# A row maximum that reaches all partitions through ScalarE copies and a vector transpose, in a gated attention kernel

## The chip, the core and the metric

The kernel runs on one core of a Trainium2 chip. A core has five engines that run their own instruction streams side by side: TensorE (PE, matrix products into PSUM banks), VectorE (DVE), ScalarE (ACT), GpSimd (POOL) and SyncE (SP, which here only issues DMA transfers). Each stream is executed in its order; semaphores make one engine wait for another. The metric is the device time of one execution in microseconds (us), as the median of several runs.

## The reference

All data are float32. `x` is 2048 x 640, with 32 heads of width 128; `W` is 512, so each head sees the last 512 keys.

```
xn = layernorm(x)
q  = xn @ wq                                  # 32 heads
p  = softmax(q k^T * Dh**-0.5)                # k, v: the last 512 rows of the cache
s  = (p v) @ wo
h  = relu(xn @ w1 + b1) ** 2                  # 640 -> 1728
g  = silu(h @ w2 + b2)
return x + s * g
```

## The kernel before

Every matrix product is made of three: each operand is split into a high part, rounded to the matmul's input type, and the low remainder, and high x high, high x low and low x high are summed (`triple`). So each tensor that goes into a product needs a rounding copy (on ACT) and a subtraction (on DVE or POOL).

The kernel first runs the norm and the MLP of the gate (`first_step` over 14 chunks of the hidden width for the first of four row tiles, then pairs of chunks for two more, then the products with `w2`); pieces that are needed later are stored to DRAM ("spills": `xT_d`, `ts_d`, the gate `g_d`, the hidden tiles `h_m`). The fourth row tile's MLP is computed at the end (`late_*`).

Then comes attention: 128 **units**, one for each pair of a head and a tile of 512 rows; `hf` counts two halves of 64 units, each with two row tiles, and in the second half the projection of q is computed with fewer products by sums of weight blocks. For unit `i`:

- `s_mm`: scores, transposed: four PSUM banks `s` (one for 128 keys each), 128 keys on the partitions, 512 rows along the free axis. The four banks serve one unit at a time.
- `max_fold`: the maximum over the keys. DVE reads each bank transposed in blocks of 32x32 and takes the maximum over 32 keys; the result `rdm` holds, on 4 x 32 partitions, partial maxima. `gather` copies three groups of 32 partitions to the first (ACT), and `row` reduces them to 32x16, `rowm`.
- In the kernel before, SP then stores `rowm` to DRAM (`m_d`) and loads it back onto all 128 partitions (`bm`, 128x512).
- `shift`: `e = s - bm`, four instructions on DVE, which free the banks of `s`.
- `expo` and `p_hi` (ACT), `p_lo` (POOL) twice each, for two halves of 128x1024 in `e`: the exponential and its two parts `pt`.
- `s_add` (POOL) adds the two halves of `e`, `s_fold` (DVE, `rds`) reduces them over keys; gather, `sq`, its reciprocal and a transpose `rows` follow. This row goes through DRAM too (`s_d`, `bs`), before and after the change.
- `v_mm`: the product with v, into `o`; `o_norm` multiplies by `bs`; `o_hi` and `o_lo` split the result into `ot`.
- Every second unit the heads' outputs are multiplied by `wo` in five blocks (`r_mm`), and `r_acc` adds them to `acc` on DVE.

The order is written out by hand. The calls of all units are put into one list, `plan`, each with a planned time (`on(10.4 + 0.4 * c, shift, i, c)` means 10.4 us after the unit's start, units being 12.4 us, `PERIOD`, apart); the list is sorted by that time and executed, and each engine runs its instructions in exactly that order. So a number in the list sets only the order on an engine, not a time. `BM` and `BS` are the planned times within a unit for DMA issues on SP.

After the last unit the rest of the fourth tile's MLP runs, mixed with the finishing of the second half's outputs: `load_finish` loads a gate tile `fg` and an input tile `fx` (two buffers each), `finish_gate` multiplies on DVE, `finish` adds on POOL or DVE and, before the change, stores the output on SP's queue at once.

Of the kernel before, what the change touches and what calls it, by code (L numbers as in the profile page):

```python
# [25 lines left out]
def kernel(  # L26
# [729 lines left out]
    def first_step(f):  # L756
# [142 lines left out]
    def raw_tile(kind, name):  # L899
        if "fin" in pools and kind in "vsxgw":  # L900
            n = D if kind == "w" else W
            return pools["fin"].tile(
                [P, n], F32, tag=f"fin{kind}", name=name, bufs=1 if kind in "vw" else 2
            )
# [225 lines left out]
    def max_fold(i, c):  # L1130
        if c == 0:
# [3 lines left out]
            SC[i, c].rearrange("p (i b) -> p b i", i=B32),  # L1135
# [10 lines left out]
    def row(i, what):  # L1146
        rd = RD.pop((i, what))[:B32].rearrange("p b a c -> p b (a c)")
        r = ap.tile([B32, B32], F32, tag="row", name=f"row{what}{i}", bufs=4)
        if what == "m":
            r = r[:, :NQ]  # L1150
            dve.tensor_reduce(r, rd, axis=AX.X, op=ALU.max)
        else:
            sq = SQ[i % len(SQ)]
            dve.tensor_reduce(sq[:, :NQ], rd, axis=AX.X, op=ALU.add)
            dve.reciprocal(sq[:, :NQ], sq[:, :NQ])
            dve.transpose(r, sq)
            r = r[:NQ]
# [4 lines left out]
        (MB if what == "m" else RB)[i] = bc  # L1162
# [319 lines left out]
    for p in range(1, NP):  # L1482
# [142 lines left out]
    BM, BS = 4.4, 11.9  # L1625
    for n in range(NG):
# [13 lines left out]
        for k, lo, what, *places in (  # L1640
# [8 lines left out]
            (3, 2, "s4", (2, BM), (2, BS)),  # L1649
# [5 lines left out]
    for t in range(TPH):  # L1655
        at((b - 5 + t * G) * PERIOD + 4.3, open_xT, 1, t)
    for u, when, pieces in (
# [3 lines left out]
        (-5, BM, ((0, 2),)),  # L1661
        (-5, BS, ((0, 3),)),
        (-4, BM, ((0, 0),)),
        (-4, BS, ((0, 1),)),
        (-3, BM, ((0, 4),)),
        (-3, BS, ((1, 0), (1, 1))),
        (-2, BM, ((1, 2),)),
        (-2, BS, ("t31", (1, 3))),
        (-1, BM, ((1, 4),)),
        (-1, BS, ("t40", "t41x")),  # L1670
# [39 lines left out]
    for i in range(NU):  # L1710
# [21 lines left out]
        if NG <= n < HALF * NG:  # L1732
# [29 lines left out]
            if n > NG:  # L1762
                at(t0 - PERIOD + 4.4, q_piece, n, slot)
# [15 lines left out]
        on(PERIOD + 8.5, row, i, "s")  # L1779
        on(18.6, p_lo, i, 1)  # L1780
        for c in range(KC):
            on(PERIOD + 8.5 + 0.68 * c, v_mm, i, c)
        on(2 * PERIOD + (4.15 if i >= NQS and i % UPG == UPG - 2 else 3.6), o_norm, i)
        on(2 * PERIOD + 4.9, o_hi, i)
        on(2 * PERIOD + 5.5, o_lo, i)
        if i % G == G - 1:
            for d in range(DC):
                last = i == NU - G - 1
                if i < NU - 1:
# [14 lines left out]
                    if k == "x" and round(when % PERIOD, 2) in (7.5, 7.75) and not last:  # L1804
                        done = when - when % PERIOD + 12.5
                    on(done, r_acc, i, d)
                if g == NG - 1 and hf == 0:
                    at((i + ((4, 4, 5, 5, 5), (4, 4, 4, 5, 5))[t][d]) * PERIOD + 4.3, store_acc, t, d)
                    w = (NU // 2 + 9 + 4 * d) * PERIOD
                    if t == 0:  # L1810
# [3 lines left out]
                        at(w + 3 * PERIOD - 0.7, finish, 0, t, d)  # L1814
    z = (NU - 1) * PERIOD
# [92 lines left out]
    at(z - 3 * PERIOD + 4.3, open_xT, HALF, 0)  # L1908
    for c in range(DC):
        for i in range(2):  # L1910
            when = ((4.5, 11.9), (16.9, 16.95), (24.3,) * 2, (24.3,) * 2, (29.2,) * 2)[c][i]
# [56 lines left out]
```

## Time and profile before

| | us |
|---|---|
| three timed runs | 2039.5, 2040.52, 2040.64 |
| median | 2040.52 |
| profiled execution | 2033.68 |
| its span, first to last instruction | 2031.9 |

| engine | busy share of the span |
|---|---|
| POOL | 67% |
| ACT | 62% |

The profile is one execution. A line of its order in time gives the start, the length, the engine, the operation with "written tile <- read tiles", and in brackets how long the engine had stood idle before and what released it. Attention fills the stretch from about 300 to 1930 us. The granted TensorE clock is 0.992 over the span.

### The profile page before, as it was taken

How to read it: one execution, taken by the hardware profiler on the slowest of the kernel's cores; microseconds unless marked ns; L12 is line 12 of the kernel's file. 1: busy time of each engine (PE TensorE's matmuls, PEld its weight loads, DVE VectorE, ACT ScalarE, POOL GpSimd, SP SyncE). 2: the span in 40 equal slices, each digit the busy share in tenths (PEclk: the TensorE clock that was granted, in tenths of full speed). 3: DMA queues.
4: the chain of work that ended last, by engine and by line, in shares of the span. 5: the costliest groups of instructions: out<-in, count | busy, mean ns of one | idle time of the engine just before them, and what ended most of it. 6: DMA issues, size and time to landing. Idle time of an engine off the chain costs nothing.

```text
span 2031.9 us, 29531 instructions
## 1 busy us (share of the span) xinstructions
PE 1961.2 (97%) x8489; PEld 1586.2 (78%) x8489; DVE 1638.8 (81%) x2851; ACT 1249.6 (62%) x2226; POOL 1368.6 (67%) x771
## 2 busy tenths in 40 slices
PE   9999999999999999999999999999999999999977
PEld 7887887788888888877877777777777777777765
DVE  6873747898989988899888778888888888888753
ACT  5665537766666666666665576666666666666522
POOL 1022108888888888888886677777777777777631
PEclk9999999999999999999999999999999999999988
DMA  6567945444444444444444544444444444444363
GB/s 211 189 236 270 360 170 169 138 142 141 137 136 139 141 141 137 146 146 146 136 147 136 177 135 143 143 143 142 140 123 123 123 126 126 128 125 140 110 221 130
DMA packets 196126, 315.57 MB, mean 155 GB/s; under 512 B 28212, under 2 KB 85062, under 8 KB 194694
## 3 DMA queue, kind: packets, MB, share of 16 engines
q1 hardware_dynamic: 192102, 297.54, 46.8%
q0 software_dynamic: 3728, 15.99, 2.0%
q8 instruction: 77, 1.26, 0.2%
q14 instruction: 75, 0.61, 0.1%
q10 hardware_dynamic: 144, 0.16, 0.0%
HBM read 243.08 MB, written 70.53 MB: 154 GB/s over the span
## 4 chain that ended last, share of the span: by engine, by line
PE 41%; DMA 20%; DVE 18%; POOL 10%; ACT 6%; issue 4%; SPq 1%; DVEq 0%; ACTq 0%; POOLq 0%
DMA bm<-m_d 9%; PE r L78 7%; PE pq L78 7%; PE py L78 7%; PE s L78 7%; DVE e L78 6%; POOL pt L78 6%; PE o L78 5%; DVE rdm L78 4%; POOL e L78 4%; DMA m_d<-rowm 4%; PE ph L78 3%; DMA bs<-s_d 2%; DVE acc L78 2%; ACT pt L78 2%
## 5 line engine op out<-in xcount | busy, mean ns | idle before, releaser
L78 POOL TENSOR_TENSOR pt<-e,pt 128x1024 fp32r<-128x1024 f32 x256 | 615.6, 2405 | 271.7 <-ACT pt L78 271.1
L78 PE MATMUL r<-ot,wo 128*128 128x512 f32 x1920 | 492.7, 390 | 2.6 <-DVE acc L78 1.7
L78 ACT ACTIVATE e<-e 128x1024 f32<-128x1024 f32 x256 | 269.5, 1053 | 262.0 <-DVE e L78 256.7
L78 PEld LDWEIGHTS r<-ot,wo 128*128 128x128 f32 x1920 | 360.3, 188 | 80.2 <-DVE acc L78 3.0
L78 PE MATMUL s<-q,wk 128*128 128x512 f32 x1536 | 375.4, 393 | 27.2 <-DVE e L78 26.7
L78 PE MATMUL o<-pt,wv 128*128 128x512 f32 x1536 | 381.8, 393 | 7.1 <-POOL pt L78 4.3
L78 DVE TENSOR_TENSOR e<-s,bm 128x512 f32<-128x512 f32 x512 | 317.1, 680 | 73.6 <-DMA bm<-m_d 68.4
L78 PEld LDWEIGHTS s<-q,wk 128*128 128x128 f32 x1536 | 284.1, 188 | 103.8 <-issue 32.3
L78 PEld LDWEIGHTS o<-pt,wv 128*128 128x128 f32 x1536 | 284.3, 188 | 83.4 <-POOL pt L78 26.1
L78 DVE TRANSPOSE_TENSOR_REDUCE rdm<-s 128x16 f32<-128x512 f32 x512 | 324.3, 685 | 5.0 <-PE s L78 4.9
L78 POOL TENSOR_TENSOR e<-e,e 128x1024 f32<-128x1024 f32 x128 | 308.6, 2411 | 10.0
L78 ACT ACTIVATE pt<-e 128x1024 fp32r<-128x1024 f32 x256 | 271.8, 1062 | 6.9
L78 PE MATMUL pq<-ax,wq 128*128 128x512 f32 x960 | 228.0, 389 | 0.0
L78 PEld LDWEIGHTS pq<-ax,wq 128*128 128x128 f32 x960 | 180.2, 188 | 37.4
L78 DVE TRANSPOSE_TENSOR_REDUCE rds<-e 128x32 f32<-128x1024 f32 x128 | 159.5, 1246 | 58.6 <-POOL e L78 58.1
L78 DVE TENSOR_TENSOR acc<-r,acc 128x512 f32<-128x512 f32 x300 | 201.8, 673 | 3.1 <-PE r L78 3.0
L78 ACT ACTIVATE rdm<-rdm 32x64 f32<-32x64 f32 x384 | 97.8, 255 | 133.5 <-DVE rdm L78 130.1
L78 ACT ACTIVATE rds<-rds 32x32 f32<-32x32 f32 x384 | 90.0, 234 | 82.1 <-DVE rds L78 77.7
L78 POOL TENSOR_TENSOR wo<-or,wo 128x640 fp32r<-128x640 f32 x62 | 104.9, 1691 | 8.0 <-ACT wo L78 7.9
L78 DVE TENSOR_TENSOR o<-o,bs 128x512 f32<-128x512 f32 x128 | 87.3, 682 | 21.3 <-DMA bs<-s_d 20.6
L78 PE MATMUL py<-ch,cw 128*128 128x512 f32 x410 | 95.9, 395 | 4.8 <-ACT r L78 4.8
L78 DVE TENSOR_TENSOR ot<-o,ot 128x512 fp32r<-128x512 f32 x128 | 86.9, 679 | 15.6 <-ACT ot L78 14.3
(460 smaller groups left out, 2492.6 us busy)
## 6 DMA issues: line engine op xcount, KB each, us to landing
bm<-m_d SPq DMA_DIRECT2D x128, 256.0 KB
bs<-s_d SPq DMA_DIRECT2D x128, 256.0 KB
or<-in_wo_dram SPq DMA_DIRECT2D x62, 320.0 KB
qp<-wq_d SPq DMA_DIRECT2D x30, 640.0 KB
kr<-in_kT_dram SPq DMA_DIRECT2D x62, 256.0 KB
vr<-in_v_dram SPq DMA_DIRECT2D x62, 256.0 KB
wq_d<-ss SPq DMA_DIRECT2D x60, 256.0 KB
qp<-wq_d SPq DMA_DIRECT2D x30, 512.0 KB
```

Source lines behind the costliest of these rows:

```text
L78: ins = method(*args, **kwargs)
```

## The change

Three things are changed.

First, the maximum no longer goes through DRAM. `row` writes `rowm` into the first 32 of 128 partitions; three ACT copies (`copies`) repeat it on the other three groups of 32; and one DVE instruction (`across`) transposes, in 32x32 blocks, a 128x512 pattern in which each of the 16 columns is read 32 times, so that every partition ends with all 512 maxima. The block order that `max_fold` reads is changed to fit.

Second, the planned times in the list are changed around this: the subtractions, exponentials and copies come earlier, the fold of the sum moves ahead of the row of the maximum, and the split of `o` and some loads and stores of projection weights (`BM`, `BS`) move.

Third, the spills of the MLP's inputs (`xT_d` of two tiles) are issued earlier, only part of the second is spilled, and the temporary sums `ts_d` are spread over four steps; the output stores are taken out of `finish` and put later into the list.

```
-        if p in (2, 3):
-            spill(p - 1, XS[p - 1])
-        for k in {1: (0,), 4: (1, 2), 5: (3,)}.get(p, ()):
+        if p < NP - 1:
             for i in range(2):
-                pool.dma_start(TS_d[k][:, :, i, :], raw(TS[k][i]))
+                pool.dma_start(TS_d[p - 1][:, :, i, :], raw(TS[p - 1][i]))
...
+        if f in (9, 10):
+            pool.dma_start(xT_d[T1][f - 9], raw(XS[T1][f - 9]))
+        if f == FC - 1:
+            cs = slice(NQ2, DC)
+            for i in range(2):
+                pool.dma_start(xT_d[T2][i][:, cs, :], raw(XS[T2][i])[:, cs, :])
...
-            SC[i, c].rearrange("p (i b) -> p b i", i=B32),
+            SC[i, c].rearrange("p (b i) -> p b i", i=B32),
...
     def row(i, what):
         rd = RD.pop((i, what))[:B32].rearrange("p b a c -> p b (a c)")
+        if what == "m":
+            r = MR[i] = ap.tile([P, NQ], F32, tag="rowm", name=f"rowm{i}", bufs=2)
+            dve.tensor_reduce(r[:B32], rd, axis=AX.X, op=ALU.max)
+            return
...
+    def copies(i):
+        for a in range(1, P // B32):
+            act.activation(MR[i][a * B32 : (a + 1) * B32], MR[i][:B32], AF.Copy)
+
+    def across(i):
+        MB[i] = ap.tile([P, NT], F32, tag="bm", name=f"bm{i}", bufs=1)
+        dve.transpose(
+            MB[i].rearrange("p (b i) -> p b i", i=B32),
+            MR.pop(i)[:, :, None].to_broadcast([P, NQ, B32]),
+        )
...
         (pool if t == hf else dve).tensor_tensor(a, a, FX.pop(("x", hf, t, d)), op=ALU.add)
-        store(sp, hf, t, d, a)
+        FX["o", hf, t, d] = a
+
+    def finish_store(hf, t, d):
+        store(sp, hf, t, d, FX.pop(("o", hf, t, d)))
...
-    BM, BS = 4.4, 11.9
+    BM, BS = 0.85, 4.5
...
         on(3.95, gather, i, "m")
         on(4.1, row, i, "m")
+        on(4.25, copies, i)
+        on(7.0, across, i)
         for c in range(KC):
-            on(10.4 + 0.4 * c, shift, i, c)
-        on(11.7, expo, i, 0)
-        on(12.7, p_hi, i, 0)
-        on(13.8, expo, i, 1)
-        mid = i >= NQS and i % UPG == UPG - 1
-        on(PERIOD + (4.0 if mid else 5.2), p_hi, i, 1)
-        on(13.9, p_lo, i, 0)
-        on(16.2, s_add, i)
-        on(PERIOD + 6.2, s_fold, i)
-        on(PERIOD + 8.0, gather, i, "s")
-        on(PERIOD + 8.5, row, i, "s")
-        on(18.6, p_lo, i, 1)
+            on(8.2 + 0.6 * c, shift, i, c)
+        on(9.5, expo, i, 0)
+        on(10.6, p_hi, i, 0)
+        on(10.7, expo, i, 1)
+        on(10.9, p_hi, i, 1)
+        on(11.0, p_lo, i, 0)
+        on(11.1, s_add, i)
+        on(11.2, p_lo, i, 1)
+        on(PERIOD + 3.5, s_fold, i)
+        on(PERIOD + 4.15, gather, i, "s")
+        on(PERIOD + 4.4, row, i, "s")
...
-        on(2 * PERIOD + (4.15 if i >= NQS and i % UPG == UPG - 2 else 3.6), o_norm, i)
+        on(2 * PERIOD + 4.2, o_norm, i)
         on(2 * PERIOD + 4.9, o_hi, i)
-        on(2 * PERIOD + 5.5, o_lo, i)
+        on(2 * PERIOD + (7.6 if i < NU - 1 else 5.5), o_lo, i)
...
             at(z + 36.0 + 4.0 * t + 8.0 * d, finish, HALF - 1, t, d)
+            at(z + 46.0 + 4.0 * t + 8.0 * d, finish_store, HALF - 1, t, d)
```

The matmuls on PE stand in the same order before and after. On DVE, in the first half, this stood between the fold of the sum of unit 27 (`rds27`) and the first two subtractions of unit 28 (`e28_0`); the digits after the tile's name are the unit, then the half of `e` or the bank of `s`:

```order
L78 TENSOR_REDUCE rds27_6962<-e27_0_6875 128x2x16
L78 SCALAR_TENSOR_TENSOR q30_1_6977<-pq30_6943,q30_0_6976 128x512
L78 TENSOR_REDUCE sq3_2985<-rds27_6962 32x16
L78 RECIPROCAL sq3_2985<-sq3_2985 32x16
L78 STREAM_TRANSPOSE rows27_6992<-sq3_2985 32x32
L78 TENSOR_TENSOR e28_0_7014<-s28_0_6893,bm28_6940 128x512
L78 TENSOR_TENSOR e28_0_7014<-s28_1_6902,bm28_6940 128x512
```

In the changed kernel the same place on DVE reads:

```order
L78 TENSOR_REDUCE rds27_6967<-e27_0_6877 128x2x16
L78 TENSOR_REDUCE rowm28_6972<-rdm28_6941 32x16
L78 TENSOR_TENSOR acc0_0_3561<-r25_1_6959,acc0_0_3561 128x512
L78 TENSOR_TENSOR o26_6889<-o26_6889,bs26_6848 128x512
L78 TENSOR_REDUCE sq3_2985<-rds27_6967 32x16
L78 RECIPROCAL sq3_2985<-sq3_2985 32x16
L78 STREAM_TRANSPOSE rows27_6986<-sq3_2985 32x32
L78 STREAM_TRANSPOSE bm28_7005<-rowm28_6972 128x512
L78 TENSOR_TENSOR ot26_6994<-o26_6889,ot26_6994 128x512
L78 TENSOR_TENSOR e28_0_7019<-s28_0_6931,bm28_7005 128x512
L78 SCALAR_TENSOR_TENSOR q30_1_7017<-pq30_6982,q30_0_7016 128x512
L78 TENSOR_TENSOR e28_0_7019<-s28_1_6937,bm28_7005 128x512
```

`rowm`, `acc`, `o` and `ot` have moved from ahead of `rds` to behind it, `bm` is new, and the second part of q has moved between the two subtractions.

On ACT, in the second half, this stood between the exponential of unit 92's second half and that of unit 93's first:

```order
L78 ACTIVATE e92_1_15806<-e92_1_15806 128x1024
L78 ACTIVATE rdm93_15824<-rdm93_15824 32x16x4 x3
L78 ACTIVATE ot91_15869<-o91_15786 128x512
L78 ACTIVATE pt92_1_0_15871<-e92_1_15806 128x1024
L78 ACTIVATE q94_0_15884<-pq23b_15637 128x512
L78 ACTIVATE q95_0_15888<-pq23a_15790 128x512
L78 ACTIVATE rds92_15881<-rds92_15881 32x16x2 x3
L78 ACTIVATE wv1_13_0_15902<-vr1_13_15798 128x512
L78 ACTIVATE e93_0_15927<-e93_0_15927 128x1024
```

In the changed kernel ACT's order there is:

```order
L78 ACTIVATE e92_1_15892<-e92_1_15892 128x1024
L78 ACTIVATE pt92_1_0_15908<-e92_1_15892 128x1024
L78 ACTIVATE rdm93_15924<-rdm93_15924 32x16x4 x3
L78 ACTIVATE rds92_15949<-rds92_15949 32x16x2 x3
L78 ACTIVATE rowm93_15960<-rowm93_15960 32x16 x3
L78 ACTIVATE ot91_15978<-o91_15881 128x512
L78 ACTIVATE q94_0_15986<-pq23b_15739 128x512
L78 ACTIVATE q95_0_15990<-pq23a_15887 128x512
L78 ACTIVATE wv1_13_0_16006<-vr1_13_15899 128x512
L78 ACTIVATE e93_0_16004<-e93_0_16004 128x1024
```

The gather of the sum (`rds92`) and the three new copies of `rowm93` now stand ahead of `ot91` and of the first parts of q.

More of the change, by code (lines that the diff above doesn't have):

```diff
@@ L902, in raw_tile @@
             return pools["fin"].tile(
-                [P, n], F32, tag=f"fin{kind}", name=name, bufs=1 if kind in "vw" else 2
+                [P, n], F32, tag=f"fin{kind}", name=name, bufs={"v": 1, "w": 3}.get(kind, 2)
             )
@@ L1147, in row @@
         rd = RD.pop((i, what))[:B32].rearrange("p b a c -> p b (a c)")
+        if what == "m":
+            r = MR[i] = ap.tile([P, NQ], F32, tag="rowm", name=f"rowm{i}", bufs=2)
+            dve.tensor_reduce(r[:B32], rd, axis=AX.X, op=ALU.max)
+            return
         r = ap.tile([B32, B32], F32, tag="row", name=f"row{what}{i}", bufs=4)
[L1149 to L1157, printed above, removed]
+        sq = SQ[i % len(SQ)]
+        dve.tensor_reduce(sq[:, :NQ], rd, axis=AX.X, op=ALU.add)
+        dve.reciprocal(sq[:, :NQ], sq[:, :NQ])
+        dve.transpose(r, sq)
+        r = r[:NQ]
         d = dpool.tile(list(r.shape), F32, tag=f"{what}_d", name=f"{what}_d{i}", bufs=4)
@@ L1161, in row @@
         sp.dma_start(bc, d.rearrange("a b -> (a b)")[None, :].to_broadcast([P, NT]))
-        (MB if what == "m" else RB)[i] = bc
+        RB[i] = bc
+    MR = {}
+    def copies(i):
[7 more added lines that the diff above has]
+        )
     def shift(i, c):
@@ L1660 @@
         (-14, BM, ("t30",)),
[L1661 to L1670, printed above, removed]
+        (-5, BS, ((0, 2),)),
+        (-4, BM, ((0, 3),)),
+        (-4, BS, ((0, 0),)),
+        (-3, BM, ((0, 1),)),
+        (-3, BS, ((0, 4), (1, 0))),
+        (-2, BM, ((1, 1),)),
+        (-2, BS, ("t31", (1, 2))),
+        (-1, BM, ("t41x", (1, 3))),
+        (-1, BS, ("t40",)),
+        (0, BM, ((1, 4),)),
         (1, BS, ("t41",)),
```

13 lines of the change are left out of this document (6 added, 7 removed).

## The prediction

> **What bounds the kernel now.** I read the busy shares first, then the waits, then the order in time of one unit of attention (a head times a tile of 512 rows; 128 of them follow one another). "L78" is the line of a wrapper through which every instruction is issued, so I go by tile names: `s` scores, `rdm`, `rowm`, `bm` the maximum in its three forms, `e` exponentials, `pt` their two parts, `rds`, `sq`, `rows`, `bs` the sum, `o`, `ot` the head's output, `acc` the accumulator, `sw` sums of projection weights.
>
> ```profile
> PE 1961.2 (97%) x8489; PEld 1586.2 (78%) x8489; DVE 1638.8 (81%) x2851; ACT 1249.6 (62%) x2226; POOL 1368.6 (67%) x771
> DVE rds L78 <- POOL e L78: 58.1, 103, 3.0
> DVE e L78 <- DMA bm<-m_d: 68.4, 75, 3.5
> PE s L78 <- DVE e L78: 26.7, 30, 2.2
> 404.60:1003.80 599.20, 72.59 (x96) 1.00 0.46 141
> 1184.30:1786.30 602.00, 72.57 (x96) 1.00 0.43 133
> ```
>
> TensorE is at 97%, so one would look no further. But VectorE (DVE) waits 103 times for POOL and 75 times for the maximum from DRAM. The last two rows are windows for the tile `rds` on DVE: two instructions per unit have that name, so 96 are 48 units: **12.48 us a unit in the first half, 12.54 in the second**. One unit in the order of time, all engines:
>
> ```profile
> 1007.46 2.48 DVE L78 TENSOR_TENSOR e<-s,bm 128x512 f32<-128x512 f32 x4 [0.77 <-DMA bm<-m_d]
> ...
> 1008.84 1.07 ACT L78 ACTIVATE e<-e 128x1024 f32<-128x1024 f32 x1 [1.68 <-DVE e L78]
> 1008.97 2.88 PE L78 MATMUL s<-q,wk 128*128 128x512 f32 x12
> ...
> 1009.94 1.06 ACT L78 ACTIVATE pt<-e 128x1024 fp32r<-128x1024 f32 x1
> ...
> 1011.08 2.40 POOL L78 TENSOR_TENSOR pt<-e,pt 128x1024 fp32r<-128x1024 f32 x1 [1.40 <-ACT pt L78]
> ...
> 1013.56 2.40 POOL L78 TENSOR_TENSOR e<-e,e 128x1024 f32<-128x1024 f32 x1
> ...
> 1016.00 1.25 DVE L78 TRANSPOSE_TENSOR_REDUCE rds<-e 128x32 f32<-128x1024 f32 x1 [0.49 <-POOL e L78]
> 1017.16 0.65 DVE L78 SCALAR_TENSOR_TENSOR q<-pq,q 128x512 fp32r<-128x512 f32 x1
> 1017.27 0.72 ACT L78 ACTIVATE rds<-rds 32x32 f32<-32x32 f32 x3 [0.40 <-DVE rds L78]
> ...
> 1019.21 2.48 DVE L78 TENSOR_TENSOR e<-s,bm 128x512 f32<-128x512 f32 x4
> ...
> 1021.21 2.88 PE L78 MATMUL s<-q,wk 128*128 128x512 f32 x12
> ```
>
> This is a **loop**. Two subtractions, the exponential, its rounded copy, POOL's remainder, POOL's sum, then the fold `rds`: 1016.00 - 1007.46 = 8.54 us. DVE is in order, so the next unit's subtractions come only after that fold: 1019.21 - 1016.00 = 3.21 us. The loop here is 11.75 us against 12.24 for PE (1021.21 - 1008.97). Both are near the 12.48 measured: there is almost no room in it, and the question is what the change puts into it.
>
> **The change, in the loop.** The order shows that `rowm` and `o` and `ot`, which stood ahead of `rds`, now stand behind it; the new wide transpose `bm` is there too, and one more instruction stands between the first two subtractions. So all of them lie between one unit's fold and the next unit's exponential, in the loop. What each takes from start to start (DVE alone):
>
> ```profile
> 942.30 0.67 DVE L78 TENSOR_TENSOR acc<-r,acc 128x512 f32<-128x512 f32 x1
> 942.90 0.25 DVE L78 TENSOR_REDUCE sq<-rds 32x16 f32<-32x128 f32 x1
> 943.18 0.24 DVE L78 RECIPROCAL sq<-sq 32x16 f32<-32x16 f32 x1
> 943.46 0.20 DVE L78 STREAM_TRANSPOSE rows<-sq 32x32 f32<-32x32 f32 x1
> 943.59 0.62 DVE L78 TENSOR_TENSOR sw<-qr,qr 128x256 f32<-128x256 f32 x1
> ...
> 952.19 0.41 DVE L78 TENSOR_REDUCE rowm<-rdm 32x16 f32<-32x256 f32 x1 [0.27 <-ACT rdm L78]
> 952.53 0.67 DVE L78 TENSOR_TENSOR acc<-r,acc 128x512 f32<-128x512 f32 x1
> 953.12 0.67 DVE L78 TENSOR_TENSOR ot<-o,ot 128x512 fp32r<-128x512 f32 x1
> ...
> 957.60 2.48 DVE L78 TENSOR_TENSOR e<-s,bm 128x512 f32<-128x512 f32 x4 [0.39 <-DMA bm<-m_d]
> 960.00 0.68 DVE L78 TENSOR_TENSOR acc<-r,acc 128x512 f32<-128x512 f32 x1
> ```
>
> So `sq` 0.28, reciprocal 0.28, small transpose 0.13, `rowm` 0.34, and every instruction over 128x512 0.60 (acc 942.30 to 942.90, and 2.40 for four e); `rds` 1.16 (1016.00 to 1017.16).
>
> The **price of the new transpose** is in no row. Bounds: the small transpose and the fold of 128x1024, which reads twice as much. I take 0.60, that of the nearest width, and keep 0.13 to 1.16 for the range. The three ACT copies of `rowm` are no larger than those of `rdm`:
>
> ```profile
> L78 DVE STREAM_TRANSPOSE rows<-sq 32x32 f32<-32x32 f32 x128 | 25.5, 200 | 4.7 <-DVE sq L78 0.2 <-DMA wq_d<-wq 0.2
> L78 ACT ACTIVATE rdm<-rdm 32x64 f32<-32x64 f32 x384 | 97.8, 255 | 133.5 <-DVE rdm L78 130.1
> L78 ACT ACTIVATE ot<-o 128x512 fp32r<-128x512 f32 x128 | 75.5, 590 | 30.9 <-DVE o L78 30.0
> L78 ACT ACTIVATE q<-pq 128x512 fp32r<-128x512 f32 x64 | 38.0, 593 | 39.5 <-PE pq L78 39.4
> ```
>
> Now the walk, from the start of `rds` at 0. On ACT, in its new order: gather of the sum 1.27 to 2.00 (1017.27, 0.72), copies of `rowm` to 2.76, `ot` to 3.35, `q` to 3.94 where it is next. On DVE, first half, unit 28: `rowm` 1.16, `acc` 1.50, `o` 2.10, `sq` 2.70, reciprocal 2.98, `rows` 3.26, `bm` 3.39 (its copies ended at 2.76, no wait), `ot` 3.99, **e at 4.59**. In every other unit `acc` is not there but the second part of q stands between `bm` and `ot`: it waits for ACT's q until about 4.0, and e comes at 5.2. Mean 4.90. From e to the next fold it was 8.54; with the instruction between the first two subtractions it is 9.14. **Loop: 14.04 us**, with about equal numbers of either kind. DVE's other work in the unit (two subtractions, an acc, four folds of the maximum, about 4.4 us) fits into the 7.16 us between exponential and fold, and PE's 12.24 fits too.
>
> Second half, four kinds of unit by the order, nearly equal in number: one more q ahead of e (5.19), two q, the first of which waits for ACT (6.4), none (4.59), and mostly a projection sum right behind `rds` (5.03 on average). Mean 5.30, **loop 14.44 us**.
>
> Against the measured units: (14.04 - 12.48) x 63 + (14.44 - 12.54) x 64 = 98 + 122 = **220 us more**. What goes away, the wait for `bm` from DRAM (68.4 us), is already in these sums, as the walk has no such wait. The 256 DMA issues and the 256 KB per unit that leave SP's queue are worth nothing more. The added wait is DVE's for POOL's sum ahead of `rowm`: behind it stand the `acc` that free PE's banks, `o` and the new maximum, and PE waits for all of them. The longer wait for `bs` is covered: its store is issued a whole loop before `o` reads it.
>
> **The change outside the loop.** The earlier spills leave less traffic while the middle of the MLP writes its hidden tiles, and the output stores no longer stand on SP ahead of the loads that the end of the kernel needs.
>
> ```profile
> PE py L78 <- ACT r L78: 4.8, 2, 2.5
> PE lu L78 <- POOL l1w L78: 12.9, 3, 6.6
> PE ly L78 <- ACT l2w L78: 5.1, 2, 3.5
> DVE acc L78 <- DMA fg<-g_d: 26.8, 6, 5.7
> ```
>
> The first wait (`py`, behind ACT's r) can at most go: 0 to 4.8, I take 4. At the end PE waits for l1w because POOL first has to finish an output that DVE could not start for want of `fg`; 0 to 18.0 (12.9 + 5.1) could go, I take 12, since the tiles of `fg` and `fx` still have only two buffers. The re-timed loads and stores of projection weights (`BM`, `BS`) move on SP beside a PE that waits for none of them in the rows above: nothing, and if that cover goes, they wait inside a unit that DVE holds up anyway.
>
> **Sum.** The profiled execution took 2033.68 us (span 2031.9), the median of the timed runs is 2040.52, 6.84 more. 2033.7 + 220 - 4 - 12 = 2237.7; as a median of runs **2245 us**, 10% slower.
>
> **Rivals.** *Faster* (0.07): the loop does not lengthen, because POOL's sum is always there before the fold is reached, the DRAM wait and PE's 26.7 us are gained, and PE's 12.24 becomes the pace: 0.24 x 63 + 0.30 x 64 = 34 us less, and 16 for the rest: 2033.7 - 34 - 16 + 6.8 = 1990. It decides at a loop of 12.5 us; the walk would have to be wrong by 1.5 us a unit, and the row of 1016.00 shows that DVE waits for POOL even now, with a shorter loop. *No change* (0.03): the same loop about 1.4 us shorter than my walk, so that 16 us of gain outside stand against the rest: 2040. That the change doesn't do what it says is excluded by the order, which has no `m_d` left.
>
> *Slower still* (0.08): the wide transpose is held up by POOL, which works most of the time. DVE instructions of one shape show such a thing:
>
> ```profile
> L78 DVE TENSOR_TENSOR sw<-sw,qr 128x256 f32<-128x256 f32 x16 | 21.5, 1343 | 0.5
> L78 DVE TENSOR_TENSOR sw<-qr 128x256 f32<-128x256 f32 x16 | 6.4, 398 | 0.0
> ```
>
> 1343 ns against 398 for the same size. At 0.95 us a unit it adds 0.95 x 127 = 121: 2366 us. Against it: the 128 small transposes took 200 ns on average, so hardly any of them was held. [...]
>
> **Chances and range.** Forecast 0.82, slower still 0.08, faster 0.07, no change 0.03. The transpose alone moves the sum by -0.47 x 127 = -60 or +0.56 x 127 = +71, the end of the kernel by +12 or -6. Range 2185 to 2335. Within 0.2% is about what a measurement of this kernel cannot tell from no change: faster 0.07, same 0.03, slower 0.90.
>
> **What would show it.** In the changed profile the wait of `rds` for POOL's e should be near 2 us a unit, some 250 to 300 us in all, and no longer half a microsecond; PE's share should fall to about 88%, with waits at `s` or `o`; e to fold should be 9.1 us and fold to e 4.6 to 6.4; the `bm` row should read some 0.65 to 0.7 us. If `rds` does not wait, or stands elsewhere in time, the forecast is wrong. If PE's wait for l1w remains, the term of 12 is.

## The result and the profile after

The changed kernel takes 2214.23 us (median of four runs, 2212.74 to 2215.43) against 2040.01 us of the kernel before on the same chip: a ratio of **1.0858, interval 1.084 to 1.0877**. The profiled execution took 2214.28 us, its span is 2212.5; that of the kernel before, on which the prediction worked, took 2033.68 us, 6.3 less than its median.

The busy row, the waits, and the windows for the tile `rds` on DVE, as shown of before:

```profile
PE 2028.0 (92%) x8489; PEld 1608.9 (73%) x8489; DVE 1706.1 (77%) x2979; ACT 1322.4 (60%) x2610; POOL 1353.5 (61%) x771
DVE rds L78 <- POOL e L78: 215.6, 117, 3.7
PE o L78 <- DVE ot L78: 65.6, 44, 3.8
PE r L78 <- DVE acc L78: 64.9, 37, 2.4
404.60:1003.80 599.20, 64.78 (x86) 0.98 0.34 108
1184.30:1786.30 602.00, 63.16 (x84) 0.96 0.32 102
```

No engine is busier than 92%, and VectorE, which should have gained from the shorter way of the maximum, now stands idle 215.6 us in front of `rds` alone. The windows hold 86 and 84 instructions that have to do with `rds`, two a unit, where before held 96: 599.20 / 43 = 13.93 us and 602.00 / 42 = 14.33 us a unit, against 12.48 and 12.54. A window counts whole instructions, so such a quotient can be wrong by one unit in 42, some 0.3 us. The starts of `rds` over each whole half give it more closely: 12.52 and 12.73 us a unit in before, 13.92 and 14.60 here.

One unit of the first half on DVE, in the order of time (start, length, what ran, and in brackets the idle time ahead of it):

```profile
1101.76 1.25 DVE L78 TRANSPOSE_TENSOR_REDUCE rds<-e 128x32 f32<-128x1024 f32 x1 [3.03 <-POOL e L78]
1102.93 0.36 DVE L78 TENSOR_REDUCE rowm<-rdm 32x16 f32<-32x256 f32 x1
1103.22 0.67 DVE L78 TENSOR_TENSOR acc<-r,acc 128x512 f32<-128x512 f32 x1
1103.82 0.68 DVE L78 TENSOR_TENSOR o<-o,bs 128x512 f32<-128x512 f32 x1
...
1105.13 0.66 DVE L78 STREAM_TRANSPOSE bm<-rowm 128x512 f32<-128x512 f32 x1
1105.72 0.64 DVE L78 TENSOR_TENSOR ot<-o,ot 128x512 fp32r<-128x512 f32 x1
1106.29 0.66 DVE L78 TENSOR_TENSOR e<-s,bm 128x512 f32<-128x512 f32 x1
...
1113.64 0.65 DVE L78 TENSOR_TENSOR acc<-r,acc 128x512 f32<-128x512 f32 x1
1115.41 1.25 DVE L78 TRANSPOSE_TENSOR_REDUCE rds<-e 128x32 f32<-128x1024 f32 x1 [1.11 <-POOL e L78]
```

From `rds` to the next subtraction 1106.29 - 1101.76 = 4.53 us, from there to the next `rds` 9.12. In the unit shown of before these were 3.21 and 8.54; over all units of the first half the means are 3.96 and 8.56 in before, 4.80 and 9.13 here. The wait in brackets is the loop closing: DVE has run out of work and stands until GpSimd has added the halves of `e`, and everything behind `rds` in its order stands with it, the `acc` and `ot` for which TensorE waits in the rows above.

Where the time went, by the scores of the first and the last unit (the row of `s` on PE, its last numbers before the shape being the first and last start), first of before, then of after:

```profile
L78 PE MATMUL s<-q,wk x1536: 387/389/504, 297.3 to 1899.0; 128*128 128x512 f32 x192
```

```profile
L78 PE MATMUL s<-q,wk x1536: 387/389/507, 289.8 to 2098.0; 128*128 128x512 f32 x192
```

Attention from first to last scores: 1601.7 us before, 1808.2 after, **206.5 more**. The part ahead of it became 7.5 us shorter (297.3 to 289.8), the part behind it 18.4 (2031.9 - 1899.0 = 132.9 against 2212.5 - 2098.0 = 114.5). Together +180.6, the difference of the spans.

### The profile page after: what moved, and what is told of

It is laid out like the page before. It is cut to its first block, busy times and chain, and to the rows that moved or that the text cites. A ratio compares the mean times of both kernels' runs of the same rounds, so it can differ in the third digit from the quotient of the medians.

```text
span 2212.5 us, 29675 instructions
## 1 busy us (share of the span) xinstructions
PE 2028.0 (92%) x8489; PEld 1608.9 (73%) x8489; DVE 1706.1 (77%) x2979; ACT 1322.4 (60%) x2610; POOL 1353.5 (61%) x771
## 4 chain that ended last, share of the span: by engine, by line
PE 30%; POOL 23%; DVE 16%; ACT 15%; issue 12%; DMA 2%; POOLq 0%; SPq 0%; ACTq 0%; DVEq 0%
POOL e L78 11%; POOL pt L78 10%; PE py L78 6%; PE o L78 5%; PE r L78 5%; ACT pt L78 5%; ACT e L78 4%; DVE e L78 4%; PE s L78 4%; PE ph L78 3%; DVE acc L78 2%; DVE q L78 2%; DVE rds L78 2%; PE wa L78 2%; DVE ot L78 1%
## 5 line engine op out<-in xcount | busy, mean ns | idle before, releaser
L78 PE MATMUL r<-ot,wo 128*128 128x512 f32 x1920 | 515.4, 402 | 66.0 <-DVE acc L78 64.9
L78 PE MATMUL o<-pt,wv 128*128 128x512 f32 x1536 | 410.9, 419 | 65.6 <-DVE ot L78 65.6
L78 PEld LDWEIGHTS o<-pt,wv 128*128 128x128 f32 x1536 | 306.7, 203 | 157.0 <-issue 43.1
L78 DVE TRANSPOSE_TENSOR_REDUCE rdm<-s 128x16 f32<-128x512 f32 x512 | 340.3, 703 | 48.4 <-PE s L78 48.3
L78 DVE TENSOR_TENSOR e<-s,bm 128x512 f32<-128x512 f32 x512 | 328.5, 670 | 0.1
L78 DVE TRANSPOSE_TENSOR_REDUCE rds<-e 128x32 f32<-128x1024 f32 x128 | 159.2, 1244 | 215.6 <-POOL e L78 215.6
L78 DVE TENSOR_TENSOR acc<-r,acc 128x512 f32<-128x512 f32 x300 | 202.3, 674 | 70.0 <-PE r L78 69.5
L78 POOL TENSOR_TENSOR wv<-vr,wv 128x512 fp32r<-128x512 f32 x62 | 79.9, 1289 | 86.5 <-ACT wv L78 86.5
L78 POOL TENSOR_TENSOR wo<-or,wo 128x640 fp32r<-128x640 f32 x62 | 97.9, 1579 | 28.6 <-ACT wo L78 28.6
L78 POOL TENSOR_TENSOR ss<-sw,ss 128x256 fp32r<-128x256 f32 x64 | 47.4, 742 | 110.2 <-ACT ss L78 96.7
L78 POOL TENSOR_TENSOR wk<-kr,wk 128x512 fp32r<-128x512 f32 x60 | 78.2, 1304 | 52.5 <-ACT wk L78 52.5
```

What stands on the lines that cost most here:

```text
L78: ins = method(*args, **kwargs)
```

## The experiments

Twelve kernels. Each ratio is against runs of the kernel before on the same chip.

### The edges of the kernel alone

**Spills, stores and the buffers of `w`, on the kernel before.** Attention is that of before, word for word. The third part of the change also gives the tile `w` three buffers in place of one, which the description of the change ahead of the prediction doesn't name: `w` takes the raw weights `l1r` from which `l1w` is made at the end.

```diff
+        if f in (9, 10):
+            pool.dma_start(xT_d[T1][f - 9], raw(XS[T1][f - 9]))
...
-                [P, n], F32, tag=f"fin{kind}", name=name, bufs=1 if kind in "vw" else 2
+                [P, n], F32, tag=f"fin{kind}", name=name, bufs={"v": 1, "w": 3}.get(kind, 2)
...
+            at(z + 46.0 + 4.0 * t + 8.0 * d, finish_store, HALF - 1, t, d)
```

> The kernel before, with only the third part of the change: the earlier and smaller spills of the MLP's inputs, and the output stores put later into the list. Prediction's step: these two parts gain by themselves, 7.5 us up to the first score (297.3 to 289.8) and up to 18 us behind the last one (132.9 to 114.5): about 2040 - 22 = 2018 us. Rival: the gain at the end came from the slower attention stage, which left loads more time; then only the 7.5 us at the start remain, 2032 us.

Measured: 2011.54 us, ratio 0.9847 (0.9826 to 0.9867). Its row of scores:

```profile
L78 PE MATMUL s<-q,wk x1536: 387/389/763, 290.8 to 1899.3; 128*128 128x512 f32 x192
```

So the edges are a gain, and the whole of the loss lies in attention: 1808.2 against 1608.5 us here.

**The spills alone, and the stores with the buffers of `w`**, on the kernel before.

> The kernel of before with the earlier and smaller spills alone. The run with spills and stores gave 2011.5 us against 2040.6, with the first s 6.5 us earlier and the stretch after the last s 21.3 shorter. If the spills give the head alone: 2034, the last stretch still 133. If the spills also clear GpSimd's queue for the last loads (lu waited 12.9 us for l1w and then 1.7 to 2.9): 2012 to 2022.

Measured: 2032.81 us, 0.9965 (0.9952 to 0.9978); first scores at 290.0, and the wait for l1w stays:

```profile
PE lu L78 <- POOL l1w L78: 12.9, 3, 6.6
```

> The kernel of before with the later output stores and the third buffer of w alone. If the stores give the last stretch: 2019, the first s at 297 and the last stretch 112. If they give nothing because the last stretch is set by GpSimd's load of l1w, which they don't move: 2040, last stretch 133.

Measured: 2015.47 us, 0.9885 (0.987 to 0.9899); first scores at 298.2, the last stretch 2012.6 - 1902.8 = 109.8 us, and

```profile
PE lu L78 <- POOL l1w L78: 1.2, 2, 0.8
```

The two add up: -6.7 and -24.0 against 2039.49, together -30.7, and -29.1 for both at once. The spills give the head, the other run the tail, where TensorE's wait for l1w, which POOL prepares, goes. That run has two edits, the later stores and the three buffers of the tile that l1w is made from, and no run has one without the other. The traces speak for the stores: at the end of before SP waited 45.1 us for outputs that POOL and DVE had yet to write (28.5 and 16.6) and only 1.6 us for a buffer behind l1w; in this run it waited 16.2 us for outputs, DVE's wait for the gate tile `fg` fell from 26.8 to 3.4 us, and POOL's wait for DVE's product, which stands ahead of its l1w, from 43.9 to 20.9.

The stretch behind the last scores became 23.1 us shorter (132.9 to 109.8), which is more than the waits that went (11.7 at l1w, 3.9 at ly). The windows of that stretch show the rest (length, then busy time of PE, PEld, DVE, ACT and POOL, the granted clock, DMA share, GB/s), first of before, then of the run with the stores:

```profile
1899.00:2031.90 132.90, 109.25 (x448) 85.99 (x446) 67.85 (x90) 44.72 (x73) 45.99 (x29) 0.92 0.49 154
```

```profile
1902.80:2012.60 109.80, 101.78 (x448) 81.18 (x446) 68.25 (x90) 44.51 (x73) 45.72 (x29) 1.00 0.58 186
```

The same 448 matmuls take 7.47 us less at a clock of 1.00 in place of 0.92: **the waits that were taken from TensorE paid a second time here**. 11.7 + 3.9 + 7.5 is the 23.1. In the head it is the same in small: from 108 to 298 us TensorE was busy 185.17 of 190 us at a clock of 0.98 in before, and 190.00 at 1.00 with the spills alone.

### The loop, from inside the changed kernel

**The wide transpose twice.** The second writes the same values again.

```diff
-        dve.transpose(
+        for _ in range(2):
+            dve.transpose(
```

> The changed kernel with the wide transpose done twice, the second time writing the same values. Loop theory: 0.60 us more where the chain runs through the transpose; in the units where the next instruction waits for ACT's q anyway (fold to e 5.0 us, about half of the first half) it hides in that wait of 0.4 us for the most part, and adds 0.2. So 0.6 x 96 + 0.2 x 31 = 64 us, about 2278 us. Work theory: DVE gets 0.6 us more in each of 128 units, 77 us, 2291 us. If DVE's idle time (23% of the span) can take up work anywhere: 2214 us.

Measured: 2291.41 us, 1.1219 (1.12 to 1.1239), 77.2 above the changed kernel. Two instructions of DVE and the next `rds`:

```profile
597.81 1.25 DVE L78 TRANSPOSE_TENSOR_REDUCE rds<-e 128x32 f32<-128x1024 f32 x1 [1.36 <-POOL e L78]
...
603.10 0.67 DVE L78 TENSOR_TENSOR e<-s,bm 128x512 f32<-128x512 f32 x1
...
612.21 1.25 DVE L78 TRANSPOSE_TENSOR_REDUCE rds<-e 128x32 f32<-128x1024 f32 x1 [3.04 <-POOL e L78]
```

`rds` to e is 5.29 here and 5.27 in the next unit, where the changed kernel has 5.04 in units with a q behind `bm` and 4.53 in those without (with a q, a part of the second transpose lies in the wait for ScalarE's q). From e to `rds` it is 9.11, as in the changed kernel. First to last scores grew by 1887.6 - 1808.2 = 79.4 us, 0.63 a unit (by the starts of `rds`, 0.51 in the first half and 0.74 in the second). DVE stood idle 1.4 to 3 us ahead of `rds` in these units, yet the added work went into the time nearly in full: that idle time is not room, since the work stands behind it in the loop. The theories of the loop (64 us) and of plain work on DVE (77) lie close together here, and the time came out at the second; the run rules out that the idle time absorbs the work, and doesn't decide between the two.

**The four subtractions in one run**, so that no q stands between the first two.

```diff
-            on(8.2 + 0.6 * c, shift, i, c)
+            on(8.2 + 0.01 * c, shift, i, c)
```

> The changed kernel with the four subtractions of a unit next to each other in DVE's order (planned 0.01 us apart, not 0.6). No work is added or removed. Loop theory (one unit's fold of the sum, the row of the maximum, the transpose, the subtractions, the exponential, POOL's sum, the next fold): the 0.60 us of the instruction between the first two subtractions leaves the loop; e to fold falls from 9.12 to about 8.54 us, the unit by 0.58 us, the time by 0.58 x 127 = 74 to about 2140 us. Work theory (the extra instructions on DVE and ACT cost their own length wherever they stand): the same work, so 2214 us. Bank theory (PE waits 65 us for the acc instructions that free its banks, and that sets the pace): the acc instructions come later, so 2214 us or more.

Measured: 2190.75 us, 1.0729 (1.0711 to 1.0748), 23.5 us below the changed kernel: far less than the loop promised. The windows for `rds`:

```profile
404.60:1003.80 599.20, 66.54 (x90) 1.00 0.35 110
1184.30:1786.30 602.00, 62.68 (x84) 0.94 0.31 101
```

The first half did most of what was expected: 45 units where there were 43, and by the starts of `rds` 13.47 us a unit, 0.45 less where 0.58 was promised. The second half did not move (42 units as before, 14.67 us a unit by the starts): in this window its units take 12.6 to 16.7 us, with stretches from e to `rds` of up to 10.85, as in the changed kernel. DVE's two largest waits in the whole run:

```profile
DVE rds L78 <- POOL e L78: 151.8, 84, 3.9
DVE acc L78 <- PE r L78: 121.7, 76, 4.0
```

In the changed kernel the first was 215.6 and the second 69.5, of which 62.5 lay in the second half; here 41.4 us of it are new in the first. So the loop is what binds in the first half, with the wait of `acc` for TensorE's `r` close behind it. In the second half that wait was there already; it points to a ring of DVE and TensorE, each late for the other, but no run separates that from the lower clock there (0.94).

**The fold of the sums late**, directly ahead of the subtractions (8.1 in place of 3.5), its gather and row behind it: GpSimd's sum is then always ready.

```diff
-        on(PERIOD + 3.5, s_fold, i)
+        on(PERIOD + 8.1, s_fold, i)
```

> The changed kernel with the fold of the sum put right ahead of the next unit's subtractions (planned time 8.1 in place of 3.5), its gather behind it and its row behind the second subtraction. All instructions stay. Loop theory: rowm, acc, o, sq, bm and ot leave the loop; what is left is the fold 1.16 and e to fold 9.12, 10.3 us, less than PE's 12.24, so PE sets the pace with about 12.3 us in both halves: 2214 - (13.93 - 12.3) x 63 - (14.33 - 12.3) x 64 = about 1980 us, faster than the kernel before (2040). The wait of rds for POOL goes to almost nothing. Work theory: the same work, so still about 2200 us. Transpose theory (the way through ACT copies and the transpose is itself too slow for a unit): at best a part of it comes back, 2100 us or more.

Measured: 2108.94 us, 1.0334 (1.0315 to 1.0353). The wait of `rds` for GpSimd is gone from the list, and 105 us of the 203 above the run with the edges alone with it, but not all: the loop theory's 1980 is missed by 129. What stands in its place, in one unit of the first half, first DVE and then POOL:

```profile
657.45 0.64 DVE L78 TENSOR_TENSOR e<-s,bm 128x512 f32<-128x512 f32 x1
658.02 1.56 DVE L78 TENSOR_TENSOR sw<-qr 128x256 f32<-128x256 f32 x1
659.61 2.46 DVE L78 TENSOR_TENSOR sw<-sw,qr 128x256 f32<-128x256 f32 x1
661.99 0.68 DVE L78 TENSOR_TENSOR e<-s,bm 128x512 f32<-128x512 f32 x1
```

```profile
657.71 1.59 POOL L78 TENSOR_TENSOR wq<-qr,wq 128x640 fp32r<-128x640 f32 x1
659.26 2.53 POOL L78 TENSOR_TENSOR pt<-e,pt 128x1024 fp32r<-128x1024 f32 x1
```

Each sum of query weights ends 0.28 us after the GpSimd instruction beside it (658.02 + 1.56 = 659.58 against 659.30, 662.07 against 661.79). The fourth subtraction waits behind them, and with it the second exponential. In this stretch units without such sums took 11.71 to 13.35 us, those with them 13.49 to 16.28, this one the longest, and DVE stands idle for less than 1 us of it: it is full. The second half has no such sums, and its units still took 13.10 us; what holds them there no run shows.

**The late fold with the subtractions in one run**, to take the sums of query weights from between them. The row of the sum (`sq`, its reciprocal, `rows`) stays between the second and the third.

> The late fold with the four subtractions in one run. The run with the late fold alone gave 2108.9 us: there the units with a DVE sum of query weights between two subtractions lasted 13 to 16 us, because the sum (sw<-sw,qr, mean 2335 ns, against some 420 where nothing held it) stood ahead of the fourth subtraction while GpSimd worked. Theory now (no loop is left; what binds is DVE's own order with sums that GpSimd slows): with nothing between the subtractions the two exps and GpSimd's work no longer wait for the slow sums, those units come to about 12.5 to 13, and the kernel to 1990 to 2050. Rival (DVE is simply full, whatever the order): 2090 to 2110 again.

Measured: 2213.26 us, 1.0855 (1.0839 to 1.0871): a miss, 104 us the wrong way. **And with the sums of query weights directly behind the subtractions**, and the row of the sum behind those, which is a second move in the same run:

> As the run before it, and the sums of query weights moved to directly behind the four subtractions, where GpSimd waits for the exp and rounded copy of ScalarE. Theory (GpSimd holds DVE's operations with two inputs in SBUF): sw rows come from 1400 to 2300 ns mean to 400 to 700, and the time falls by the difference, about 1 to 3 us for each of the units that have them, 10 to 60 us below the run before. Rival (the sums are slow for another reason, their own data or DMA): the rows stay above 1200 ns and the time within 10 us of the run before.

Measured: 2267.44 us, 1.1113 (1.1083 to 1.1143): a second miss. The sums did become shorter (`sw<-sw,qr` 1573 ns after 2377), but by far less than expected, since GpSimd's next instruction was already there (in one unit `wq<-qr,wq` from 640.77 to 642.50, and the sum beside it from 641.13 to 642.78). A part of the loss was q. In this run, first DVE and then PE:

```profile
643.42 0.64 DVE L78 SCALAR_TENSOR_TENSOR q<-pq,q 128x512 fp32r<-128x512 f32 x1
647.07 0.69 DVE L78 TENSOR_TENSOR acc<-r,acc 128x512 f32<-128x512 f32 x1 [3.02 <-PE r L78]
```

```profile
644.11 2.92 PE L78 MATMUL r<-ot,wo 128*128 128x512 f32 x6 [4.31 <-DVE q L78]
```

TensorE's products `r` wait 4.31 us for DVE to have read the bank of q, and then DVE's next `acc` waits 3.02 us for `r`: two in-order engines, each waiting for what stands late in the other's queue. In this run `PE r` waited 108.5 us for q in all, in the one before 72.0, and with the subtractions apart the wait is not in the list.

**The same with q ahead of the subtractions**, where it had stood behind them.

```diff
-            on(q_at + low, q_lo, n)
+            on(8.15 if abs(q_at + low - 8.4) < 0.01 else q_at + low, q_lo, n)
```

> The late fold with the subtractions in one run (2213.3 us) and the queries' rounding remainder (DVE q) ahead of the subtractions instead of behind them, in the units where it stood there. Theory (in that run the queue of DVE made q late, TensorE waited 2.1 and 3.15 us for it in the units shown, and the accumulations behind it waited for TensorE): those waits go, PE r <- DVE q falls from 72 us to below 20, and the kernel comes to 2090 to 2150. Rival (DVE is full with the sums that GpSimd holds, and q's place is only the place where the excess shows): the wait moves to another row and the time stays within 20 us of 2213.

Measured: 2164.6 us, 1.0619 (1.0602 to 1.0635). `PE r` no longer waits for q, as expected, and 49 us went; the time fell short of the range, since other waits took a part of it (`PE pq` for `acc` 52.2 us, 20.4 with q behind the subtractions). So q's place explains about half of the miss of 104. The sums of query weights are still long (`sw<-sw,qr` 2373 ns in the mean); whether they make the other half no run shows. These four runs settle that a late fold alone doesn't repair the order; they don't give the best order.

### The path alone, in the order of before

**Copies and transpose in place of the way through DRAM, all else as before**, on the kernel with the new edges. The transpose stands directly ahead of the subtractions.

```diff
         on(4.1, row, i, "m")
+        on(4.25, copies, i)
+        on(10.3, across, i)
```

> The order of before, with its edges as in the run that changed the edges alone (2011.5 us), and of the attention's change only the path: the copies on ScalarE and the wide transpose take the place of the maximum's way through DRAM; the transpose stands directly ahead of the four subtractions, behind the fold of the sums. Every other instruction of attention keeps the place of before. Theory (the time went into the new order, not into the path): the transpose lengthens the DVE stretch from rds to the next e by 0.6 us and takes away the wait for bm out of DRAM (68.4 us in all in before, 0.53 a unit), so a unit stays within 0.2 us of 12.5 and the kernel comes to 2010 to 2040. Rival (the path costs its work in any order, 0.6 us of DVE and three copies on ScalarE a unit): 128 units by 0.6 to 1.3 us on top of 2011.5, 2088 to 2178.

**The same with the transpose ahead of `rds`** (6.1 in place of 10.3).

> The same kernel with the wide transpose ahead of the fold of the sums, where DVE waits for GpSimd about 0.5 us a unit in before. Theory: the transpose lies in that wait and outside the stretch from rds to e, so the stretch is shorter than in before by the wait for bm, and the kernel comes to 1995 to 2015, at or below the run that changed the edges alone. Rival (the path costs its work): 2088 to 2178 as in the run before it.

Measured: 2076.02 us, 1.0183 (1.0167 to 1.02), and 2070.82 us, 1.0153 (1.0132 to 1.0174). Neither theory: 64 and 59 us above the run with the edges alone, and nearly the same wherever the transpose stands, so its place does not decide. By the starts of `rds` nearly all of it lies in the first half: 13.57 and 13.50 us a unit against 12.60 there, 12.82 twice against 12.76 in the second. In the first of the two, DVE's waits, and ACT in one unit:

```profile
DVE ot L78 <- ACT ot L78: 117.4, 126, 1.4
```

```profile
631.83 0.66 ACT L78 ACTIVATE rowm<-rowm 32x16 f32<-32x16 f32 x3 [0.78 <-DVE rowm L78]
632.50 0.60 ACT L78 ACTIVATE ot<-o 128x512 fp32r<-128x512 f32 x1
633.00 1.05 ACT L78 ACTIVATE pt<-e 128x1024 fp32r<-128x1024 f32 x1
```

ScalarE's copies wait for `rowm` and hold `ot` and `pt`, which are ready, behind them. DVE's `ot` stands ahead of `rds`, so e to `rds` became 8.71 to 9.19 us in the units of this stretch.

**The copies behind `ot` and `pt`**, otherwise the first of the two.

```diff
-        on(4.25, copies, i)
+        on(5.3, copies, i)
```

> The kernel with the path in before's order (2076.0 us, the transpose ahead of the subtractions), with ScalarE's three copies of rowm moved behind its ot<-o and its second pt<-e. There the copies stood ahead of both: they waited 0.47 to 1.01 us for rowm and then ran 0.66, so DVE's ot waited 117.4 us in all for ScalarE's, and the stretch from e to rds was 8.71 to 9.19 where the run with the edges alone has 8.54. Theory (the path's cost in before's order lies in ScalarE's queue): the stretch goes back to 8.5 to 8.6, rds to e stays at 3.4 to 3.7 in units without query sums, DVE ot <- ACT ot falls below 30 us, and the kernel comes to 2000 to 2035. Rival (DVE's own 0.66 us a unit is the cost): 2060 to 2076 stays.

Measured: **2012.0 us, 0.9862 (0.9838 to 0.9885)**, 64 us less for one number in the list. The wait, ACT in a unit, DVE around its fold, and the windows for `rds`:

```profile
DVE ot L78 <- ACT ot L78: 14.3, 35, 0.7
```

```profile
629.31 0.60 ACT L78 ACTIVATE ot<-o 128x512 fp32r<-128x512 f32 x1 [0.84 <-DVE o L78]
629.93 1.06 ACT L78 ACTIVATE pt<-e 128x1024 fp32r<-128x1024 f32 x1
631.02 0.67 ACT L78 ACTIVATE rowm<-rowm 32x16 f32<-32x16 f32 x3
```

```profile
618.32 1.25 DVE L78 TRANSPOSE_TENSOR_REDUCE rds<-e 128x32 f32<-128x1024 f32 x1 [0.50 <-POOL e L78]
...
621.46 0.66 DVE L78 STREAM_TRANSPOSE bm<-rowm 128x512 f32<-128x512 f32 x1
622.15 2.48 DVE L78 TENSOR_TENSOR e<-s,bm 128x512 f32<-128x512 f32 x4
```

```profile
404.60:1003.80 599.20, 69.73 (x92) 1.00 0.38 117
1184.30:1786.30 602.00, 72.80 (x97) 1.00 0.34 112
```

Of the 64 us some 41 came back between e and `rds`, a third of a microsecond a unit in both halves. The other 23 came back between `rds` and e of the first half, where the sums of query weights stand: with the copies ahead these took longer (70.4 us for all 64 of them, 42.4 here).

In the unit shown `rds` to e is 3.83 us with the transpose in it, and the wait for `bm` from DRAM (71.9 us in the run with the edges alone) has gone in exchange. First to last scores take 1610.0 us, against 1608.5 with the way through DRAM: in sum the new path costs nothing that can be measured, and gains nothing. But the sum hides two halves. The run with the edges alone has 96 instructions in both windows. Here the first half is slower (12.88 us a unit by the starts of `rds`, against 12.60) and the second faster (12.52 against 12.76), +17 and -15 us. That fits what goes in exchange: of the wait for `bm` 22.8 us lay in the first half and 46.9 in the second, 0.36 and 0.73 us a unit, on either side of the transpose's 0.59.

### All of them

"Attention" is first to last scores of the profiled execution.

| kernel | median us | ratio to before | attention us |
|---|---|---|---|
| before | 2040.01 | 1 | 1601.7 |
| changed | 2214.23 | 1.0858 | 1808.2 |
| spills alone | 2032.81 | 0.9965 | 1606.7 |
| stores and buffers of `w` alone | 2015.47 | 0.9885 | 1604.6 |
| edges alone | 2011.54 | 0.9847 | 1608.5 |
| edges, path, copies behind | 2012.0 | 0.9862 | 1610.0 |
| edges, path, transpose ahead of `rds` | 2070.82 | 1.0153 | 1670.1 |
| edges, path, copies ahead | 2076.02 | 1.0183 | 1673.0 |
| changed, fold late | 2108.94 | 1.0334 | 1703.2 |
| changed, fold late, q ahead | 2164.6 | 1.0619 | 1759.3 |
| changed, subtractions in one run | 2190.75 | 1.0729 | 1784.7 |
| changed, fold late, subtractions in one run | 2213.26 | 1.0855 | 1810.3 |
| changed, fold late, sums early | 2267.44 | 1.1113 | 1853.1 |
| changed, two transposes | 2291.41 | 1.1219 | 1887.6 |

So the change is three things. The edges gain about 29 us. The new path is worth nothing in sum in before's order, a loss in the first half against a gain in the second, and with the copies ahead of `ot` and `pt` on ScalarE it costs 64 there. The new order of attention with that path costs about 200 against the edges alone. The runs with edges alone and with edges and well-placed path are both faster than either kernel, by 1.4 to 1.5% against before, and not told apart from each other.

## Why the prediction was right

It said 2245 us, 2185 to 2335, for the reason that the loop through `rds` lengthens. The time was 2214.23, and the loop is where the time went. Of the 30.3 us between its sum, 2244.5, and the time, 13.5 belong to the loop, 9.9 to the edges, and 6.9 to neither: 6.84 was added because the median of before lies that much above its profiled execution, and for the changed kernel the two agree (2214.23 and 2214.28). By its steps:

- **What bounds before.** It said that the loop (11.75 us) and TensorE (12.24) are both near the unit's 12.48. The last experiment agrees: with e to `rds` back at some 8.6 and `rds` to e at 4.31 in the first half and 3.88 in the second, the time is that of before's order, whichever way the maximum takes. The unit that the prediction read was a short one: with a mean `rds` to e of 3.96 the loop of before takes the unit's whole 12.5 us, not 11.75. The forecast did not rest on this, as it set the walk against the measured units.
- **The walk.** `rds` to e was forecast at 4.59 and 5.2 in the first half; the profile of after has 4.53 and, in the next unit (1120.45 - 1115.41), 5.04. From e to `rds` it was 9.14; measured 9.12. By the starts of `rds` the loops of 14.04 and 14.44 us came out at 13.92 and 14.60, in place of 12.52 and 12.73 in before: +88 and +120 us, where +98 and +122 were forecast. In the first half the walk is 0.12 us too long: 0.06 of small steps (`rowm` 0.29 and not 0.34, `ot` 0.57 and not 0.60) in one kind of unit and 0.16 in the other, where the second part of q is waited for. In the second half the four kinds of unit are there as walked (in the window of that half 5.08, 6.30, 4.49 and 4.95 us from `rds` to e, where 5.19, 6.4, 4.59 and 5.03 were forecast), but e to `rds` has a mean of 9.28 us there and not 9.14, with 9.35 and 9.61 in two of the kinds, which the walk did not tell apart. So a stretch walked too long and one walked too short nearly cancel, and that the second half came out so near is in part luck.
- **The price of the transpose.** Taken at 0.60 between 0.13 and 1.16; measured 0.59 from start to start (1105.13 to 1105.72), with this row:

```profile
L78 DVE STREAM_TRANSPOSE bm<-rowm 128x512 f32<-128x512 f32 x128 | 86.1, 673 | 0.0
```

- **The wait of `rds`.** Forecast 250 to 300 us, measured 215.6. The mechanism is right, the size was off: the working counted two subtractions, one `acc` and the folds between exponential and fold. The unit shown has a second `acc`, and 1.34 us of weight sums as well (1108.68 to 1110.02), and so less idle time.
- **TensorE's share.** Forecast about 88%, measured 92%. The same 8489 matmuls took 2028.0 us of busy time where they took 1961.2, with the granted clock down from 0.992 to 0.975: at before's busy time the share would be 1961.2 / 2212.5 = 89%. By the two clocks alone the busy time would have grown by 1.7% (0.992 / 0.975), an estimate and about half of the 3.4% that it did grow by; what the rest is, no run shows.
- **The edges.** Forecast -4 and -12, measured -7.5 and -18.4 in the changed kernel, and -6.7 and -24.0 as runs of their own. Both were mis-sized, for two reasons. The working counted TensorE's waits alone, 4.8 at most in the head and 18.0 in the tail, and left out that its clock was higher once they had gone (0.98 to 1.00, 0.92 to 1.00), worth 7.5 us in the tail. And the tail's 18.0 was cut to 12 because two buffers would still hold the gate tiles back; the wait for l1w fell from 12.9 to 1.7 all the same. The working also did not see the buffers that `w` gains.
- **The copies on ScalarE.** Counted at their length only. In the changed order that gave the right walk: DVE's `ot` stands behind `bm` there, and shows no wait for ScalarE's (1105.72). That their place in ScalarE's queue costs 64 us in before's order was in no part of the prediction.
- **The rivals.** *Faster* needed GpSimd's sum to be always there: `rds` waits for it 117 times. *Slower still* needed the transpose to be held by GpSimd: it took 656 to 712 ns in all 128 instances, 52 of which had a GpSimd instruction beside them; in the late fold 126 had, and took at most 718. What was long beside GpSimd in the late fold were the weight sums (`sw<-sw,qr` 2335 ns in the mean, 426 in the changed kernel).

Shown by runs: that the edges gain; that the path, well placed, is free in sum in before's order, so that the 200 us belong to the new order around it; that work put between `rds` and e costs about its length. Not shown by a run of its own: how much of the 200 us belongs to which of the moved instructions (`rowm`, `o`, `ot`, the q between the subtractions, the accumulations `r_acc`, of which the change also drops a delay in the list, and the loads at `BM` and `BS`). The run with the subtractions in one puts the q between them at 0.45 us a unit in the first half, and only there.

## What to carry to other kernels

When engines in order hand a unit of work round a ring, write the ring down and ask of every moved instruction whether it lands between two links of it; idle time on an engine of the ring is no room for work that stands ahead of the next link (here a second transpose there cost 77 us, with VectorE idle for 1.4 to 3 us in the units shown). A shorter path for a value (here without DRAM) buys at most the wait for that value (here half a microsecond a unit), less the work that it puts onto the engines instead (here 0.59 on VectorE), and the order that it invites can cost far more than the path. When two changes come together, measure them apart: here one part gained 29 us under another's loss of 200, and a three-instruction copy, put two places further back in its queue, was worth 64.

## What the runs showed of the hardware

- **Small instructions beside GpSimd.** `sw<-sw,qr`, 128x256 with both inputs in SBUF, took 2377 ns in the mean in the late fold with the subtractions in one run and 426 in the changed kernel, a factor of more than five. In the late fold 47 of the 64 sums took more than 0.6 us, and each of them had started while a GpSimd instruction ran and ended 0.28 to 0.29 us after that; the other 17 took at most 526 ns. The wide transpose, with one input, was never held (656 to 712 ns in the changed kernel, at most 718 in the late fold). That a hold of this size can move into the critical stretch by a change of order alone was not expected.
- **The granted clock was lower where TensorE's waits were longer, at the same busy time.** In the first half TensorE was busy 557 of 600 us both in the changed kernel and in the path with copies ahead; the clock was 0.98 in the first, whose waits there reached 2.3 us, and 1.00 in the second, where they reached 1.2. The two windows used above, taken in all fourteen kernels, fall into line by the count of TensorE's idle stretches above 2 us: none in eleven windows, all at 1.00; two or three in four, 0.99 to 1.00; ten or eleven in eight, 0.97 to 0.98; 19 to 21 in five, 0.94 to 0.97. At the end of before, with waits up to 6.6 us, it was 0.92. The longest wait alone doesn't order the rows: it was 2.2 us at 1.00 in the second half of before, 2.3 at 0.98 in the first half of the changed kernel, 3.6 (the next 2.9) at 0.96 in its second, and 4.3 at 0.97 in the second half of the late fold with sums early. No run here shows why the clock falls.
